# Band and tail loads of a bias table moved from GpSimd's queue to SyncE's, with memsets that release them, and a re-ordered opening

## The chip, the cores, the metric

The kernel runs on one core of one Trainium2 chip. The metric is device time in microseconds (us), the median of several executions. Ratios are the mean time of one kernel's fast runs over the mean of the other kernel's fast runs of the same rounds, with a 95% interval, so they are not quite the ratio of the medians. A run over 1.5% above the fastest of its kernel would count as slow and be left out.

## The reference

Attention with a relative-position bias over 8 batches, 8 heads, 576 positions and head size 64, then a bilinear feed-forward of 4608 tokens.

```python
scores = scale * q @ k.T                        # (8, 8, 576, 576)
bias = bias_table[bucket(abs(i - j))]           # 32 buckets x 8 heads
attn = softmax(scores + bias)
x = (attn @ v) reordered to (4608, 512)
out = ((x @ w_a) * (x @ w_b)) @ w_out           # 512 -> 1536 -> 512
```

## The kernel before

The bias enters as a factor: `exp(scores) * exp(bias)`. VectorE multiplies each block of exponentials by a slice of a band `W`, read backwards. The bands are built once: a small table is made on the chip, written to HBM by SyncE, and read back as overlapping rows, 128 partitions wide. For each head pair `hp` there is an upper part (`W0` to `W3`, 130 KB each) and a lower part (`R0` to `R3`, 160 KB each); `Wta` and `Wtb` (96 KB each) serve the tail, the last 64 positions.

```python
nc.sync.dma_start(out=tab.ap(), in_=tab_sb[0:H, :])          # the table to HBM

def load_w(hp, y0, y1):
    nc.gpsimd.dma_start(out=W_sb[hp][:, :, y0:y1],
                        in_=bass.AP(tensor=tab, offset=2 * hp * TB + y0,
                                    ap=[[NM, 128], [TB, 2], [1, y1 - y0]]))
def load_wt(hh):
    nc.gpsimd.dma_start(out=Wt_sb[64 * hh:64 * hh + 64, :, 64:256], in_=...)
```

The first two batches, the loads, and the first feed-forward units are placed by hand in one list, the opening. Each engine gets its instructions in the order of that list. `<x` is a load, `TK`/`TQ`/`TZ` are transpositions of keys, queries and tails, `S` scores, `E` exponentials (ScalarE), `M` products with `W` (VectorE), `AV`/`N`/`X` attention times values, its normalisation and transposition, `C..:D` or `:A` copies on VectorE or ScalarE, `KS`/`EK` the tail keys, `w` fills with zeros, `FA`/`FB` products with `w_a` and `w_b`.

```
<k0 <q0 <k1 <q123h0 <k23 <tk <W0 <v0 <W1 <vtb <vta <tq <W2 <R0 <v1 <Wta <q123h1 <W3 <Wtb <R1
<wa0 <k4 <wb0 <R2 <R3 <q4 ...
TK0 PC0:A TQ0 ... S001 PX0:D CQ01:A S000 E001 E000 ... S301 M001 TQ20 ... FA0a N01 HA0a ... FB0a
```

After the opening (about 70 us) a loop handles the other batches.

The softmax here doesn't subtract the row's maximum and nothing guards it: scores larger than these inputs give would overflow.

## Time and profile before

| | before |
|---|---|
| median of the first 3 runs | 414.07 us (412.92 to 414.61) |
| span of the profiled run | 412.2 us |
| first product with `wa` (`FA0a`) | 26.55 us |
| first product with `wb` (`FB0a`) | 29.44 us |
| first product with `w_out` | 70.65 us |

The lines of the profile, and how they were read, are in the prediction below.

### The profile page before, as it was taken

The page shows a single profiled execution, that of the slowest core. Times are in us where ns is not written, and L with a number is a line of the kernel's source. Part 1 is how long each engine was busy: PE and PEld are TensorE (multiplying, and loading weights), DVE is VectorE, ACT ScalarE, POOL GpSimd, SP SyncE. Part 2 cuts the span into 40 slices and gives each one's busy share as a digit, 9 for nine tenths or more (in the row PEclk, how much of TensorE's full clock was granted, in tenths as well). Part 3 has the DMA queues.
Part 4 walks back from the last instruction along what each step waited for, and adds up shares of the span by engine and source line. Part 5 has one row for each costly group of instructions (what it writes and reads, how often), then busy time and mean ns, then how long its engine had stood idle before and what let it go on. Part 6 is the DMA issues. An engine that isn't in the chain of part 4 may idle for free.

```text
span 412.2 us, 8768 instructions
## 1 busy us (share of the span) xinstructions
PE 404.5 (98%) x3473; PEld 210.0 (51%) x3473; DVE 240.8 (58%) x568; ACT 251.3 (61%) x384; POOL 133.6 (32%) x191
## 2 busy tenths in 40 slices
PE   8999999999999999999999999999999999999996
PEld 3576656455555455455444555555545554444443
DVE  3898997366745665476656764667547652421320
ACT  4998992676748665677556765767486642322321
POOL 6967547788029300960079004300000000000000
PEclk9999999999999999999999999999999999999999
DMA  8999999999979914995299709960520012002004
GB/s 104 179 202 189 206 166 144 160 193 142 87 133 159 139 34 91 155 129 90 41 161 143 116 16 126 127 92 17 117 67 16 17 40 78 0 9 95 2 2 102
DMA packets 135786, 42.05 MB, mean 102 GB/s; under 512 B 113688, under 2 KB 130968, under 8 KB 135744
## 3 DMA queue, kind: packets, MB, share of 16 engines
q0 software_dynamic: 81712, 20.27, 56.3%
q1 hardware_dynamic: 48592, 11.87, 18.6%
q10 hardware_dynamic: 5440, 9.34, 7.2%
q8 instruction: 27, 0.44, 0.5%
q14 instruction: 15, 0.12, 0.1%
HBM read 39.18 MB, written 9.45 MB: 118 GB/s over the span
## 4 chain that ended last, share of the span: by engine, by line
PE 94%; DVE 2%; ACT 2%; DMA 1%; issue 1%; ACTq 0%; POOL 0%; POOLq 0%
PE pb L633 23%; PE pa L633 23%; PE po L670 22%; PE av L569 8%; PE qk L406 7%; PE av L559 2%; PE av L563 2%; PE qkh L446 1%; PE qkt L479 1%; DMA qn<-in_q_dram 1%; PE trb L321 1%; ACT ath L452 1%; PE trb L415 1%; PE trb L609 0%; DVE ath L461 0%
## 5 line engine op out<-in xcount | busy, mean ns | idle before, releaser
L430 ACT ACTIVATE at<-qk 128x1024 bf16<-128x1024 f32 x112 | 113.3, 1028 | 27.5 <-DMA out_dram<-ob 10.3
L643 DVE TENSOR_TENSOR g<-pb,ha 128x512 bf16<-128x512 f32 (+1 forms) x114 | 75.6, 664 | 75.0 <-PE pb L633 58.9
L633 PE MATMUL pb<-xn,wb 128*128 128x512 bf16 (+1 forms) x456 | 112.1, 368 | 0.2 <-DVE g L643 0.2
L633 PE MATMUL pa<-xn,wa 128*128 128x512 bf16 (+1 forms) x456 | 112.1, 368 | 0.0
L640 ACT ACTIVATE ha<-pa 128x512 f32<-128x512 f32 (+1 forms) x114 | 66.2, 581 | 67.7 <-PE pa L633 66.2
L670 PE MATMUL po<-wo,g 128*128 128x512 bf16 x420 | 98.2, 379 | 0.0
L435 DVE TENSOR_TENSOR at<-at,W 128x1024 bf16<-128x1024 bf16 x112 | 75.1, 686 | 22.2 <-ACT at L430 22.1
L633 PEld LDWEIGHTS <-wa 128*128 128x128 bf16 x456 | 41.2, 98 | 46.3 <-issue 6.6
L633 PEld LDWEIGHTS <-wb 128*128 128x128 bf16 x456 | 40.6, 97 | 43.6 <-issue 5.2
L670 PEld LDWEIGHTS <-g 128*128 128x128 bf16 x420 | 38.9, 98 | 44.9 <-issue 2.5
L675 ACT ACTIVATE ob<-po 128x512 f32<-128x512 f32 x34 | 20.4, 600 | 39.9 <-PE po L670 33.6
L569 PE MATMUL av<-vm,at 128*128 128x65 bf16 x896 | 41.2, 193 | 0.0
L569 PEld LDWEIGHTS <-at 128*128 128x128 bf16 x896 | 37.4, 97 | 6.3
L132 POOL DMA_DIRECT2D qn<-in_q_dram x48 | 36.4, 807 | 12.0 <-PE qk L406 6.9
L170 POOL DMA_DIRECT2D vt<-in_v_dram x12 | 7.4, 620 | 98.9 <-PE av L563 98.1
L580 DVE RECIPROCAL rc<-av 128x6 f32<-128x6 f32 (+1 forms) x64 | 11.9, 186 | 45.2 <-PE av L569 40.8
L141 POOL DMA_DIRECT2D kn<-in_k_dram x48 | 36.2, 794 | 1.4 <-issue 0.7
L559 PE MATMUL av<-vt,att 128*128 128x130 bf16 x152 | 33.6, 221 | 0.0
L406 PE MATMUL qk<-QB,KB 64*128 64x512 bf16 x192 | 29.1, 381 | 0.0
L582 DVE TENSOR_TENSOR XG<-av,rc 128x384 bf16<-128x384 f32 (+2 forms) x64 | 27.2, 425 | 2.2
L506 ACT ACTIVATE att<-qkt 128x640 bf16<-128x640 f32 x24 | 16.8, 701 | 13.0 <-PE qkt L480 13.0
L559 PEld LDWEIGHTS <-att 128*128 128x128 bf16 x152 | 15.0, 98 | 6.5
(104 smaller groups left out, 327.0 us busy)
## 6 DMA issues: line engine op xcount, KB each, us to landing
out_dram<-ob ACTq DMA_DIRECT2D x31, 256.0 KB, 3.1
vn<-in_v_dram POOLq DMA_DIRECT2D x16, 256.0 KB, 5.8
kn<-in_k_dram POOLq DMA_DIRECT2D x48, 64.0 KB, 5.0
qn<-in_q_dram POOLq DMA_DIRECT2D x48, 64.0 KB, 4.4
wa<-in_moe_w_a_dram POOLq DMA_DIRECT2D x3, 512.0 KB, 7.4
wb<-in_moe_w_b_dram POOLq DMA_DIRECT2D x3, 512.0 KB, 9.2
wo<-in_moe_w_out_dram POOLq DMA_DIRECT2D x1, 1536.0 KB, 15.6
xn<-XG SPq DMA_TRANSPOSE x52, 3.0
```

Source lines behind the costliest of these rows:

```text
L132: nc.gpsimd.dma_start(out=by_tile(qn[b % 2])[:, h0 // 4, t, :, :], in_=q[b, h0:h1, 128 * t:128 * t + 128, :].transpose([1, 0, 2]))
L141: nc.gpsimd.dma_start(out=by_tile(kn[b % 2])[:, h0 // 4, t, :, :], in_=k[b, h0:h1, t:SM:NM, :].transpose([1, 0, 2]))
L406: nc.tensor.matmul(out=ps[:, hh, :], lhsT=kT[r, t, :], rhs=qT[r, :, :], start=True, stop=True)
L430: nc.scalar.activation(out=at[:, :, :], in_=ps[:, :, :], func=ACTF.Exp, scale=scale)
L435: nc.vector.tensor_tensor(out=at[:, :, :], in0=at[:, :, :], in1=w[:, :, S - 1 + t:S - 1 + t - SM:-1], op=MULT)
L559: nc.tensor.matmul(out=pav[:, slot, :, :], lhsT=weights_tail(p, jq), rhs=vt[i][:, :, hp, :], start=True, stop=True)
L569: nc.tensor.matmul(out=pav[:, slot, hh, :], lhsT=weights(p, t, hh, jq), rhs=vm[i][:, 2 * hp + hh, t, :], start=False, stop=True, skip_grou ...
L582: nc.vector.tensor_tensor(out=xg[:, jqs[0]:jqs[0] + m, :, :], in0=pav[:, 0:m, :, 0:Dh], in1=rc[:, 0:m, :].unsqueeze(3).to_broadcast([128, ...
L633: nc.tensor.matmul(out=ps[:, 0:n], lhsT=w[df // 4][:, mc, 128 * (df % 4):128 * (df % 4) + 128], rhs=xn_sb[mc][:, 512 * c + lo:512 * c + lo ...
L640: nc.scalar.activation(out=ha[:, 0:n], in_=ff["pa", df, lo][:, 0:n], func=ACTF.Copy)
L643: nc.vector.tensor_tensor(out=g_sb[df][:, lo:lo + n], in0=ff["pb", df, lo][:, 0:n], in1=ff["ha", df, lo][:, 0:n], op=MULT)
L670: nc.tensor.matmul(out=po[:, :], lhsT=g_sb[df][:, 128 * tt:128 * tt + 128], rhs=wo_sb[:, df, :], start=(df == 0), stop=(df == NDF - 1))
```

## The change

The intent: GpSimd should no longer stand for the table with other loads behind it. Six loads go to SyncE's queue. `W0` is issued as soon as the table has landed. The other five are released one by one: `>x` in the list writes one element of the load's destination on VectorE, and the load, which overwrites that element, must wait for the write. The place of `>x` in VectorE's order is thus the moment of release. The order of the other loads and of the opening changes too.

```diff
-    def load_w(hp, y0, y1):
-        nc.gpsimd.dma_start(out=W_sb[hp][:, :, y0:y1], ...)
+    def load_w(hp, y0, y1, eng):
+        eng.dma_start(out=W_sb[hp][:, :, y0:y1], ...)
     # the same for load_wt; W0 to W3, Wta, Wtb get nc.sync, R0 to R3 stay on nc.gpsimd
+        if token[0] == ">":
+            hp = "0123ab".index(token[-1])
+            x = Wt_sb[...1 element...] if hp > 3 else W_sb[hp][0:1, 0, 320:321]
+            nc.vector.memset(x, 1.0)
+            load(token[1:])
+            return
-        <k0 <q0 <k1 <q123h0 <k23 <tk <W0 <v0 <W1 <vtb <vta <tq <W2 <R0 <v1 <Wta <q123h1 <W3 <Wtb <R1
-        <wa0 <k4 <wb0 ...
+        <q0 <k0 <q123h0 <tk <k1 <k23 <v0 <W0 <tq <vtb <vta <R0 <v1 <q123h1 <R1 <wa0 <k4 <wb0 ...
+        TQ0 CQ00:A CQ01:A PC0:D TK0 CK0:D w1 S001 E001 S000 E000
+        TQ10 TZ1 TK1 PU0:D >W1 CQ10:D S011 CK1:D S101 E011 CZ1:D TQ20 TQ30 S100 E101 >W2 CQ20:D TK3
+        CQ30:D CK3:D TK2 CK2:D V0:D M001 E100 M100 KS EK >W3 M101 S201 E201 >Wtb M000 w2 S301 E301 w2
+        S200 >Wta M011 TZ0 S300 V1:D M201 CZ0:A AV10 ... FA0a HA0a FB0a ...
     # the rest of the list is re-ordered likewise (cut)
```

More of the change, by code (lines that the diff above doesn't have):

```diff
@@ L249 @@
     nc.vector.tensor_copy(out=tab_sb[0:H, c0:c0 + NR], in_=tps[0:H, 0:NR])
-    def load_w(hp, y0, y1):
-        nc.gpsimd.dma_start(out=W_sb[hp][:, :, y0:y1],
+    def load_w(hp, y0, y1, eng):
+        eng.dma_start(out=W_sb[hp][:, :, y0:y1],
                           in_=bass.AP(tensor=tab, offset=2 * hp * TB + y0,
@@ L257, with load_wt @@
     nc.sync.dma_start(out=tab.ap(), in_=tab_sb[0:H, :])
-    def load_wt(hh):
-        nc.gpsimd.dma_start(out=Wt_sb[64 * hh:64 * hh + 64, :, 64:256],
+    def load_wt(hh, eng):
+        eng.dma_start(out=Wt_sb[64 * hh:64 * hh + 64, :, 64:256],
                             in_=bass.AP(tensor=tab, offset=hh * TB + 512,
@@ L293, in load @@
         elif name[:2] == "Wt":
-            load_wt("ab".index(name[2]))
+            load_wt("ab".index(name[2]), nc.sync)
         elif name[0] in "WR":
-            load_w(int(name[1]), *((320, NY) if name[0] == "W" else (0, 320)))
+            load_w(int(name[1]), *((320, NY) if name[0] == "W" else (0, 320)), nc.sync if name in ('W0', 'W1', 'W2', 'W3', 'Wta', 'Wtb') else nc.gpsimd)
         else:
@@ L728 @@
     opening = """
-        <k0 <q0 <k1 <q123h0 <k23 <tk <W0 <v0 <W1 <vtb <vta <tq <W2 <R0 <v1 <Wta <q123h1 <W3 <Wtb <R1
-        <wa0 <k4 <wb0 <R2 <R3 <q4 <k5 <uq <q7 <q5 <wa1 <wb1 <k6 <uk <vt1b <k7 <vb1a <vb1b <vt1a <wa2 <q6
-        <wb2 <wo TK0 PC0:A TQ0 PF1:D PX1:D PV1:A PU0:D CK0:A CQ00:D w1 S001 PX0:D CQ01:A S000 E001 E000
-        w1 TQ30 PC1:D TK1 CK1:D TQ10 CQ10:D S011 E011 CQ30:D TK3 S100 E100 TZ1 CK3:D S301 M001 TQ20
-        PV0:D TK2 E301 S101 E101 CQ20:D CK2:D w1 S200 E200 CZ1:D M000 w1 KS w1 S201 EK w2 S010 E201 V0:D
@@ L734 @@
-        M101 TZ0 M100 M200 M201 AV00 N00 CZ0:A AV10 E010 X00 CX00:A S300 E300 N10 T0 V1:D X10 CX10:A
-        M010 ET0 AV20 TQ11 TQ21 M011 N20 CQ11:A S110 S111 CQ21:A E110 X20 M301 TQ31 M300 AV30 T1 PW:D
-        MT0 AV01 CX20:D M110 E111 N30 ET1 X30 M111 CQ31:A T2 ET2 S210 CX30:D E210 PF0:A LH FA0a N01 HA0a
-        MT1 TK4 X01 T3 AV11 ET3 CX01:D S211 PU1:D FB0a FA1a E211 CK4:D HA1a N11 X11 G0a M210 S310 MT2
-        CX11:A E310 FB1a G1a S311 FA2a HA2a TQ4 M211 CQ4:A FB2a AV21 E311 FA3a HA3a TQ5 MT3 M310 S43 S42
@@ L739 @@
-        CQ5:A G2a FB3a N21 M311 TK5 E43 E42 TZ0x G3a CZ0x:D AV31 LV CK5:D N31 FA4a HA4a X21 TQ7 CQ7:A
-        S41 E41 S52 E52 CX21:D FB4a FA5a HA5a X31 G4a TK6 M43 FB5a CX31:D S40 E40 S53 G5a FA0b FB0b
-        CK6:D M41 TZ1x HA0b G0b CZ1x:D S51 FA1b FB1b E53 M53 HA1b G1b E51 TK7 CK7:D M40 FA2b HA2b S50
-        E50 FB2b FA3b G2b HA3b V2:D T4 FB3b FA4b V3:D ET4 G3b S70 E70 M42 MT4 M52 HA4b FB4b G4b TQ6 T5
-        ET5 M50 CQ6:A AV40 N40 MT5 M51 FA5b S71 E71 HA5b S73 FB5b AV41 G5b M70 N41 S72 E73 FA6f E72 T6
@@ L744 @@
-        M73 M71 HA6f FB6f G6f AV50 N50 S62 ET6 MT6 E62 S61 FA7f HA7f M62 AV51 N51 TH S60 E61 M61 FB7f
-        G7f E60 M60 S63 E63 M63 FA8f HA8f M72 T7 FB8f G8f AV60 N60 ET7 MT7 FA9f HA9f FB9f G9f AV70 FA10f
-        FB10f N70 HA10f G10f AV71 FA11f N71 FB11f X71 HA11f G11f AV61 N61 X70 FO00 FO01 FO02 HO0 CX70:D
-        CX71:D
+        <q0 <k0 <q123h0 <tk <k1 <k23 <v0 <W0 <tq <vtb <vta <R0 <v1 <q123h1 <R1 <wa0 <k4 <wb0 <R2 <R3 <q4
+        <uq <k5 <q5 <wa1 <q7 <wb1 <k7 <uk <q6 <vb1a <k6 <vt1b <vb1b <vt1a <wa2 <wb2 <wo PC1:D PF0:A
@@ new lines @@
+        PX1:D PF1:D PX0:A PV0:D PV1:A PU1:A TQ0 CQ00:A CQ01:A PC0:D TK0 CK0:D w1 S001 E001 S000 E000
+        TQ10 TZ1 TK1 PU0:D >W1 CQ10:D S011 CK1:D S101 E011 CZ1:D TQ20 TQ30 S100 E101 >W2 CQ20:D TK3
+        CQ30:D CK3:D TK2 CK2:D V0:D M001 E100 M100 KS EK >W3 M101 S201 E201 >Wtb M000 w2 S301 E301 w2
+        S200 >Wta M011 TZ0 S300 V1:D M201 CZ0:A AV10 E200 N10 E300 AV00 N00 M200 TQ31 CQ31:A M301 S010
+        E010 M300 TQ11 TQ21 LH CQ21:A T0 CQ11:A M010 AV20 ET0 X00 N20 CX00:A S110 S111 AV30 PW:D X10 MT0
@@ new lines @@
+        E110 N30 X20 CX10:D E111 M111 T1 CX20:A AV01 N01 X30 ET1 TK4 CX30:A T2 ET2 S210 FA0a HA0a FB0a
+        M110 MT1 X01 CX01:D T3 E210 CK4:A FA1a G0a HA1a AV11 MT2 ET3 N11 S211 E211 M210 FB1a G1a FA2a
+        HA2a TQ4 X11 CQ4:A S311 E311 S310 M211 FB2a FA3a MT3 HA3a CX11:D M311 AV21 TQ5 E310 G2a TK5 N21
+        CK5:D CQ5:A S42 E42 S43 E43 M310 FB3a FA4a HA4a G3a TQ7 TZ0x CZ0x:D AV31 LV N31 S41 S52 FB4a
+        CQ7:A E41 X21 X31 FA5a G4a E52 CX21:D HA5a CX31:D FB5a S40 E40 S53 G5a FA0b HA0b FB0b M43 M52
@@ new lines @@
+        E53 TK6 TK7 G0b FA1b CK6:D M53 S51 FB1b HA1b G1b E51 FA2b HA2b TZ1x CK7:A S50 M42 E50 FB2b FA3b
+        HA3b CZ1x:D T4 G2b TQ6 M41 M40 FB3b FA4b S70 G3b ET4 V2:D HA4b MT4 FB4b T5 E70 ET5 M51 AV40 S71
+        E71 FA5b V3:D G4b N40 FB5b MT5 M50 AV41 N41 HA5b G5b S72 S73 CQ6:A FA6f AV50 E72 M71 M72 N50 T6
+        M70 E73 FB6f HA6f G6f ET6 S62 MT6 FA7f E62 M62 AV51 HA7f S61 E61 S60 N51 TH E60 M61 FB7f G7f M60
+        S63 E63 FA8f M63 T7 HA8f FB8f ET7 M73 AV60 G8f FA9f HA9f FB9f MT7 N60 AV70 FA10f G9f FB10f N70
@@ L748 @@
+        HA10f AV71 FA11f G10f FB11f N71 X71 HA11f G11f AV61 X70 N61 CX70:D FO00 FO01 FO02 CX71:D HO0
     """
@@ L757, in step @@
                     if token[1] == "a" else None)
+            return
+        if token[0] == ">":
+            hp = "0123ab".index(token[-1])
+            x = Wt_sb[64 * (hp - 4):64 * (hp - 4) + 1, 0, 64:65] if hp > 3 else W_sb[hp][0:1, 0, 320:321]
+            nc.vector.memset(x, 1.0)
+            load(token[1:])
             return
```

## The prediction

> **What bounds the kernel now.** I read the page from the whole to the part: busy times and the chain that ended last, then busy time in stretches of ten microseconds, then the waits of GpSimd, then the order of time on ScalarE, GpSimd and TensorE in the opening (the hand-written list that the change replaces; it ends near 73 us). First the whole page:
>
> ```profile
> span 412.2 us, 8768 instructions
> PE 404.5 (98%) x3473; PEld 210.0 (51%) x3473; DVE 240.8 (58%) x568; ACT 251.3 (61%) x384; POOL 133.6 (32%) x191
> PE 94%; DVE 2%; ACT 2%; DMA 1%; issue 1%; ACTq 0%; POOL 0%; POOLq 0%
> ```
>
> 94% of the chain of 412.2 us is TensorE itself. What is not TensorE is some 25 us at most, so the question is where those lie. Busy time by stretch (columns: length, PE, weight loads, DVE, ACT, POOL, granted clock, DMA share, GB/s):
>
> ```profile
> 0.00:10.00 10.00, 7.95 (x58) 3.23 (x58) 3.74 (x19) 5.14 (x8) 6.29 (x13) 1.00 0.84 103
> 10.00:20.00 10.00, 9.29 (x123) 5.27 (x120) 8.74 (x21) 8.84 (x12) 10.00 (x15) 1.00 1.17 183
> 20.00:30.00 10.00, 9.27 (x172) 7.22 (x170) 9.48 (x29) 9.03 (x14) 6.27 (x10) 1.00 1.25 196
> 30.00:40.00 10.00, 10.00 (x142) 6.97 (x140) 8.90 (x29) 8.87 (x16) 7.45 (x11) 1.00 1.38 189
> 40.00:50.00 10.00, 10.00 (x118) 6.65 (x116) 9.37 (x24) 9.48 (x17) 6.34 (x9) 1.00 1.31 204
> ```
>
> From 30 us on TensorE has no idle time at all, and the chain lies on TensorE without a break from 22.3 us. Before that it is not the bound, though its busy share looks high (matmuls overlap, and seven of them are fills with zeros). Between 10 and 26 us ScalarE and VectorE are the busy ones (88 to 95%), GpSimd issues loads without a pause from 10 to 20 us, and the DMA engines move nearly what they move later. So the opening has three near-limits: exponentials, vector work, and arrival of loads. Two waits and the issue times of GpSimd show what the change aims at (waits: total, times, longest; then its order of time: start, duration):
>
> ```profile
> POOL W L252 <- DMA bias_tab<-wo: 2.7, 1, 2.7
> POOL qn L123 <- DMA wa<-in_moe_w_a_dram: 1.8, 1, 1.8
> ...
> 8.31 0.72 POOL L252 DMA_DIRECT2D W<-bias_tab  x1 [2.66 <-DMA bias_tab<-wo]
> 9.02 0.78 POOL L123 DMA_DIRECT2D vn<-in_v_dram  x1
> 17.92 0.88 POOL L270 DMA_DIRECT2D wa<-in_moe_w_a_dram  x1
> 19.39 0.89 POOL L270 DMA_DIRECT2D wb<-in_moe_w_b_dram  x1
> ```
>
> The first load of band rows needs the bias table in HBM, which lands at 8.3 us; everything behind it on GpSimd, the v load first, stands until then. Last, ScalarE's exponentials, and TensorE where the feed-forward products begin:
>
> ```profile
> 8.01 1.94 ACT L452 ACTIVATE ath<-qkh 128x1024 bf16<-128x1024 f32 x2 [0.28 <-PE qkh L446]
> 10.79 3.05 ACT L452 ACTIVATE ath<-qkh 128x1024 bf16<-128x1024 f32 x3 [0.84 <-PE qkh L446]
> 13.99 1.94 ACT L452 ACTIVATE ath<-qkh 128x1024 bf16<-128x1024 f32 x2 [0.16 <-PE qkh L446]
> ...
> 26.55 0.61 PE L633 MATMUL pa<-xn,wa 128*128 128x256 bf16 x4
> ...
> 29.44 0.61 PE L633 MATMUL pb<-xn,wb 128*128 128x256 bf16 x4
> ```
>
> The first product needs the normalised, transposed outputs of all four head pairs for the first 256 rows. From there TensorE always has something to do. **The change can therefore gain only what it takes off the time before the first products**; the work after them is the same.
>
> **What the Trainium skill says.** "DMA: Bandwidth & Descriptors", section "Issuing engines are not separate DMA queues": loads issued from different engines share the same 16 DMA engines, and a second issuer saves only the issue time of the sequencer. The trace agrees on what an issue costs: 0.72 to 0.89 us each on GpSimd, and fifteen of them fill 10 to 20 us. The same page, "Two DMAs through the same engine are not ordered": a load that reads what another wrote must be held by the issuing engine until the first one's semaphore is full. That is the 2.7 us wait; on SyncE the wait stays but holds only SyncE. The same page, "Latency and other measured facts": the first byte comes sooner on the hardware path (about 0.6 us) than on GpSimd's (about 1 us). This trace has 1.7 us from issue to landing for small loads on SyncE against 3.1 us at best on GpSimd, but for other sizes, so it does not settle what a 130 KB band row will take.
>
> **The change part by part.**
>
> 1. *Six issues leave GpSimd* (four W, two Wt): 6 x 0.73 = 4.4 us of issue, plus the 2.7 us wait = 7.1 us. With v issued at about 5.6 instead of 9.02 us, wa0 could be issued at 17.9 - 7.1 = 10.8 us. But at most eight GpSimd loads are in flight (each waits for the one eight places before, in the built program; the 1.8 us wait on wa above is that), so wa0 (the fifteenth) waits for v, the seventh: about 13 us. Issue thus stops being the limit and arrival takes over.
>
> 2. *What arrival gains.* All the same bytes go before wa0: adding the sizes of section 6, 3272 KB up to wa0 and 3912 KB up to wb0 (k4's 128 KB and wb0's 512 KB). Before, wb0 is issued at 19.39 and lands 9.3 us later, at 28.7 us; wa0 lands at 25.3. The engines ran at 110 GB/s from 9 to 11 us, 161 from 14 to 16, and 122 from 20 to 22, against some 185 about them: (75 + 24 + 63) x 2 us = 324 KB, at 190 KB a microsecond 1.7 us, if every hole is filled. Estimate: wa0 at 23.7, wb0 at 27.0 to 27.3 us. The v load gains less: W0 and W1 now share the engines with it from 8.4 us, so I expect it at about 13 instead of 13.5 us.
>
> 3. *The order of exponentials.* The third exponential now takes the second half of pair 0, whose queries are already there, instead of waiting for pair 1; this is where the 0.84 us idle before 10.79 us goes. Adding ScalarE's work in the new order from 8.0 us to the copy that releases the first product: 12 exponentials x 0.93, tail keys 0.95, two tail exponentials x 0.9, about nine copies x 0.34 (ten at most) = 11.2 + 1.0 + 1.8 + 3.1 = 17.1 us, so 25.0 us without idle time. VectorE comes out the same: v copied by 13.8, then twelve products with the bias x 0.62, v's second half 0.7, four normalisations x 0.55, and 1.5 us of tail and copies give 24 to 25 us. First product at about 25.0 instead of 26.55: 1.5 us sooner.
>
> 4. *What the new order gives back.* In the old list some 2 us of other TensorE work (a tail product 0.4, one attention-value group 0.95, three transposes 0.3, one score group 0.3) lie between the first product with wa and the first with wb. The new list puts the wb product directly behind it. At 25.5 us wb0 has not landed by point 2, so TensorE stands until about 27.1. The product ends at 27.6, and the 1.95 us of skipped work still has to be done: 29.6 us for the state that the old kernel reaches at 29.98. Net 0.4 us if wb0 lands at 27.1; 2.0 us if it lands by 25.5.
>
> 5. *What it adds.* Five one-element memsets on VectorE, 0.06 us each by the small memsets at 1.7 us: 0.3 us of a busy engine, contained in point 3 within its error. Two fewer zero fills on TensorE, which filled waits. Both off the path.
>
> Sum: between -0.4 and -2.0 us, middle -1.2 us, a bit more for the skew towards filled holes: **412.7 us** against 414.07.
>
> **The rivals.** (a) *The loads on SyncE overtake.* Each queue gets its turn at the engines, so band rows may push back v and wa rather than fill holes. For it: DMA share over 1.1 from 11 us on. Against it: the later rows are held back by memsets behind vector work at 11 to 16 us, which is what these are for. Then the first product stays at 26.5 us or later and the time at 414 to 415. (b) *Issue was the whole limit.* If 200 GB/s are reached from 5 us on, wb0 lands by 25.5 us and ScalarE's 1.5 us and part of the fills come through: 411.5 to 412. (c) *VectorE becomes the bound.* A late W2, W3 or Wt (each gated) would stop its queue; each such stop moves the first product by its full length: up to 2 us lost, 414 to 416. (d) *Nothing moves*, because TensorE after 30 us is full anyway: it speaks only about work after 30 us; a shift of the start of the full stretch goes through to the end, so I give it little.
>
> **Range and chances.** 2% is 8.3 us. For that the full stretch would have to start at 18 us, yet ScalarE alone has 17 us of work from 8 us on; so faster by over 2% is nearly excluded. Slower by 2% needs 8 us of new waits early on, more than any load is late. The before runs spread over 1.7 us, which widens the range: 411.0 to 414.4 us. Faster 0.02, within 0.97, slower 0.01.
>
> **What would show each step right or wrong.** Point 1: GpSimd's wait on the bias table is gone ahead of v, and wa is issued at 12.5 to 14 us. Point 2: issue plus time to landing gives 23.7 for wa0 and 27 for wb0. Point 3: no idle over 0.3 us on ScalarE from 8 to 18 us, first product at 25.0. Point 4: idle time of 1 to 2 us on TensorE ahead of the first wb product, released by that load. Stretches after 40 us must look the same but for a shift. The prediction is wrong if the band rows land so late that VectorE waits for them, or if a changed stretch after 50 us (loads of batch 2, their transposes on SyncE) loses or gains time on its own.

## The result, and the profile after

The changed kernel took 415.81 us (median of 6, 414.18 to 416.17) against 413.92 us for before (6 runs): a ratio of 1.0039, interval 1.0017 to 1.0061. It is slower by 1.9 us in the medians (1.6 us by the ratio), outside the predicted range. The loss is small, but clear of the noise of these runs.

The page of after: span, busy times, and the shares of the chain that ended last.

```profile
span 414.0 us, 8724 instructions
PE 400.5 (97%) x3420; PEld 210.1 (51%) x3471; DVE 239.0 (58%) x571; ACT 251.2 (61%) x386; POOL 129.6 (31%) x185
PE 88%; DMA 4%; ACT 2%; POOL 2%; issue 2%; DVE 1%; ACTq 0%; DVEq 0%; POOLq 0%
```

TensorE's share of the chain fell from 94 to 88%, and DMA and GpSimd took some of it. The loads that this chain names are of queries and keys (2% each); the releasers in it are inferred, and the argument below rests on the waits instead. (TensorE's instruction count differs mostly because records of matmuls are missing; the weight loads, 3471 against 3473, show the two fewer fills.) By stretch (columns as in the prediction):

```profile
10.00:20.00 10.00, 8.67 (x133) 5.19 (x132) 7.64 (x23) 8.92 (x12) 6.90 (x10) 1.00 1.37 214
20.00:30.00 10.00, 6.80 (x120) 5.10 (x112) 7.13 (x20) 6.33 (x11) 4.73 (x8) 1.00 1.31 219
```

More bytes move than before (214 and 219 GB/s against 183 and 196), GpSimd is no longer full from 10 to 20 us, and yet from 20 to 30 us every compute engine does less: VectorE 7.1 us instead of 9.5, ScalarE 6.3 instead of 9.0, TensorE 6.8 instead of 9.3. What VectorE waits for from 8 to 30 us (total, times, longest):

```profile
DVE ath L461 <- DMA W<-bias_tab: 2.5, 3, 1.4
...
DVE Wt L313 <- DMA Wt<-bias_tab: 1.2, 1, 1.2
```

Before, VectorE never waited for a band row. Here are its products with the bands and the memsets that release them, in order of time:

```profile
13.99 0.69 DVE L461 TENSOR_TENSOR ath<-ath,W 128x1024 bf16<-128x1024 bf16 x1 [0.29 <-DMA W<-bias_tab]
15.51 1.31 DVE L461 TENSOR_TENSOR ath<-ath,W 128x1024 bf16<-128x1024 bf16 x2 [0.82 <-DMA W<-bias_tab]
16.15 0.06 DVE L761 MEMSET W<- 1x1 bf16 x1
16.88 0.06 DVE L761 MEMSET Wt<- 1x1 bf16 x1
...
17.60 0.06 DVE L761 MEMSET Wt<- 1x1 bf16 x1
...
22.29 1.90 DVE L461 TENSOR_TENSOR ath<-ath,W 128x1024 bf16<-128x1024 bf16 x3 [1.38 <-DMA W<-bias_tab]
...
26.02 0.23 DVE L313 COPY Wt<-Wt 128x256 bf16<-128x256 bf16 x1 [1.21 <-DMA Wt<-bias_tab]
```

`W0` costs 0.29 us, `W1` 0.82, `W3` 1.38, the tail band 1.21: together 3.70 us. The memset for `W3` stands in VectorE's order behind a product that itself waits for `W1`. It is executed at 16.15 us, and the row it releases is needed at 20.9. On TensorE the first products come to lie here:

```profile
29.44 0.61 PE L633 MATMUL pa<-xn,wa 128*128 128x256 bf16 x4
29.89 0.60 PE L633 MATMUL pb<-xn,wb 128*128 128x256 bf16 x4
```

So `FA0a` is 2.89 us later (29.44 against 26.55). From `FA0a` to the end the new list needs 384.6 us (414.03 - 29.44) against 385.6 (412.16 - 26.55): 1.0 us less. A key transposition of 0.3 us that now stands ahead of `FA0a` is a part of that; the rest was not looked into. Together they make 1.9 us of span, which is the loss. Two questions follow: why were the rows late, and is the list to blame as well?

### The profile page after: what moved, and what is told of

Read it like the earlier page. It is cut to its first block, busy times and chain, and to the rows that moved or that the text cites. A ratio compares the mean times of both kernels' runs of the same rounds, so it can differ in the third digit from the quotient of the medians.

```text
span 414.0 us, 8724 instructions
## 1 busy us (share of the span) xinstructions
PE 400.5 (97%) x3420; PEld 210.1 (51%) x3471; DVE 239.0 (58%) x571; ACT 251.2 (61%) x386; POOL 129.6 (31%) x185
## 4 chain that ended last, share of the span: by engine, by line
PE 88%; DMA 4%; ACT 2%; POOL 2%; issue 2%; DVE 1%; ACTq 0%; DVEq 0%; POOLq 0%
PE pa L633 22%; PE pb L633 22%; PE po L670 22%; PE av L569 7%; PE qk L406 7%; PE av L559 2%; DMA qn<-in_q_dram 2%; DMA kn<-in_k_dram 2%; PE av L563 2%; PE qkt L479 1%; ACT at L430 1%; PE trb L415 1%; POOL tlc L158 1%; DVE ath L461 0%; POOL kn L123 0%
## 5 line engine op out<-in xcount | busy, mean ns | idle before, releaser
L633 PE MATMUL pa<-xn,wa 128*128 128x512 bf16 (+1 forms) x440 | 110.8, 368 | 0.7
L670 PE MATMUL po<-wo,g 128*128 128x512 bf16 x403 | 95.5, 379 | 0.8
```

The costliest lines, as they stand in the source:

```text
L633: nc.tensor.matmul(out=ps[:, 0:n], lhsT=w[df // 4][:, mc, 128 * (df % 4):128 * (df % 4) + 128], rhs=xn_sb[mc][:, 512 * c + lo:512 * c + lo ...
L670: nc.tensor.matmul(out=po[:, :], lhsT=g_sb[df][:, 128 * tt:128 * tt + 128], rhs=wo_sb[:, df, :], start=(df == 0), stop=(df == NDF - 1))
```

## The experiments

Four theories. **Backlog:** the rows are late because GpSimd, freed from its wait, keeps the engines filled with up to eight loads issued earlier. **Path:** issuing such rows from SyncE is slow in itself. **Gates:** the memsets release the rows too late. **Order:** the new list is slower whatever the loads do. All experiments gave correct results. The runs of before were shared within each set (the experiments are four sets, each on another chip).

| run | median, us | before, us | ratio (95%) | `FA0a`, us |
|---|---|---|---|---|
| after | 415.81 | 413.92 | 1.0039 (1.0017 to 1.0061) | 29.4 |
| queue alone | 415.85 | 413.82 | 1.0049 (1.0030 to 1.0069) | 29.4 |
| order alone | 415.10 | 413.82 | 1.0031 (1.0013 to 1.0049) | 27.5 |
| after, no gates | 414.45 | 413.82 | 1.0016 (0.9992 to 1.0040) | 27.8 |
| after, GpSimd held | 416.26 | 413.82 | 1.0063 (1.0037 to 1.0090) | 30.7 |
| queue alone, GpSimd held | 413.68 | 414.43 | 0.9992 (0.9968 to 1.0016) | 27.1 |
| after, gates early | 413.11 | 414.43 | 0.9975 (0.9959 to 0.9992) | 26.8 |
| after, rows split | 413.95 | 414.43 | 0.9997 (0.9980 to 1.0014) | 26.8 |
| after again | 414.53 | 413.93 | 1.0031 (1.0005 to 1.0058) | 28.3 |
| order alone, loads fitted | 414.80 | 413.93 | 1.0013 (0.9999 to 1.0027) | 28.4 |
| gates early, work moved | 416.15 | 413.93 | 1.0050 (1.0036 to 1.0064) | 29.0 |
| the same, rows first | 416.46 | 413.93 | 1.0052 (1.0032 to 1.0073) | 30.0 |
| gates early again | 413.33 | 413.78 | 0.9988 (0.9968 to 1.0008) | 26.6 |

`FA0a` is from one profiled run each; the two runs of after differ by 1.1 us, so a difference of under 1 us in that column proves nothing.

### Queue alone

```diff
 # before, with:
-        nc.gpsimd.dma_start(out=W_sb[hp]...)      # W0 to W3, Wta, Wtb
+        nc.sync.dma_start(out=W_sb[hp]...)        # no memsets, list of before
```

> The list of before, word for word, with the six band and tail loads issued on SyncE and no memsets to release them. Four theories. Backlog: SyncE's rows are late because GpSimd, no longer held by the table, keeps eight loads ahead of them in the engines; then W0 takes 5 to 6 us from issue to landing here too, the first product with the bias (11.7 us in before) stands until about 13.5 to 14, and the time is 414.8 to 416. Path: SyncE's way of issuing such rows is slow in itself; same numbers here. Gates: rows are late because the memsets release them late; there are none here, so 413 to 414. Order: the new list of computations costs the time; here 413 to 414.5, like before.

`W0`, issued at 8.08 us, landed at 14.28. VectorE waited for it in one piece:

```profile
DVE ath L461 <- DMA W<-bias_tab: 3.4, 1, 3.4
```

That wait also held the key copies behind it in VectorE's order, and TensorE stood 2.8 us for one of them. The time rose by 2.0 us. So the queue alone does harm, without gates and without a new order. Backlog and path are both still possible.

### Order alone

```diff
 # after, with every row on GpSimd, no memsets:
-<k23 <v0 <W0 <tq <vtb <vta <R0 <v1 <q123h1 <R1 <wa0
+<k23 <W0 <v0 <W1 <tq <vtb <vta <W2 <R0 <v1 <Wta <q123h1 <W3 <Wtb <R1 <wa0
```

> The list of after without the memsets, all band and tail loads on GpSimd again at the relative places that they had in before (W0 ahead of the first v half, W1 behind it, and so on). Backlog, path and gates: rows land 3.1 to 4.7 us after their issue as in before, no wait of VectorE on W or Wt over 0.3 us, first product with wa at 25 to 26.5 us, time 412.3 to 414. Order: 415 to 416, as after.

A miss for the first three theories: VectorE waited for no row, but it stood 2.2 us for the second half of v and TensorE 1.9 us for queries, which the new list uses earlier than the old places deliver them. 415.10 us is what the order theory gave. (TensorE also stood 0.5 us for `wb0` here, the wait that point 4 of the prediction expected.) The new list is no gain when its loads come at the old places. It needs earlier loads, so list and load order can't be judged apart.

### After without gates

```diff
-<v0 <W0 <tq         ... >W1 ... >W2 ... >W3 ... >Wtb ... >Wta
+<v0 <W0 <W1 <W2 <W3 <Wtb <Wta <tq
```

> After, with W0, W1, W2, W3, Wtb and Wta issued on SyncE one behind the other as soon as the table has landed, no memsets. Gates: W3 and Wt have landed long before their use, the waits of 1.4 us (W3) and 1.2 us (Wt) go, and with them most of the loss: 413 to 414.3. Backlog or path: W0 and W1 come no sooner than in after (13.9 and 15.4 us), v's second half and the queries come later because more bytes go ahead of them, so half of the gain is given back: 414.5 to 415.8.

`W0` landed at 13.77 us (13.90 in after), `W3` at 17.89, the last tail row at 19.77, and no wait on a row over 0.3 us remained. In their place VectorE waited 1.2 us for v (18.47 us instead of 17.10) and TensorE 1.6 us for the queries (19.83 instead of 18.46). `FA0a` came 1.6 us sooner than in after; the median of 414.45 lies between the two forecasts, and the interval includes 1. Rows released all at once push back other loads, so gates have a use. Whether it is their place that is wrong, a later run tests.

### After with GpSimd held

```diff
+        if name == "hold":     # 16 dead bytes that need the table
+            nc.gpsimd.dma_start(out=hold_sb[:, :], in_=bass.AP(tensor=tab, offset=0, ap=[[8, 1], [1, 8]]))
     # hold_sb's own line and a return are cut here
-<k23 <v0 <W0 <tq
+<k23 <hold <v0 <W0 <tq
```

> After, with one dead load of 16 bytes of the table put on GpSimd ahead of the first v half, so that GpSimd stands until the table has landed, as it did in before; band rows stay on SyncE with their memsets. Backlog: W0 now meets nearly empty engines and lands 3 to 4 us after its issue (by 11 to 11.8 us instead of 13.9), W1 by 12.7; VectorE's waits on W0 and W1 go, v comes at about 13.5; time 414.3 to 415.3. Path: W0 still takes 6 us, and v is late on top: 416 or more.

This tells backlog from path. `W0` was issued at 8.20 and landed at 11.12 us (2.9 us), `W1` at 11.53. The packets that started, by queue (q0 is GpSimd's, q1 SyncE's; the share adds up the times of packets that overlap, so it can pass 100%), first for after from 8.0 to 10.8 us, where two rows had been issued at 7.83 and 8.28 (and a third at 10.76):

```profile
## 3 DMA queue, kind: packets, MB, share of 16 engines
q0 software_dynamic: 871, 0.42, 125.8%
```

then for after with GpSimd held, from 8.2 to 11.1 us:

```profile
## 3 DMA queue, kind: packets, MB, share of 16 engines
q0 software_dynamic: 411, 0.19, 54.6%
q1 hardware_dynamic: 539, 0.26, 37.5%
...
W<-bias_tab SPq DMA_DIRECT2D x3, 130.0 KB, 2.9
```

In after not one packet of SyncE's rows started in 2.8 us, while 871 of GpSimd's did; the first started at 11.13 us, 3.3 us after the issue. With GpSimd held the first started at 9.24 us, 1.0 us after the issue. The path theory falls, the backlog stands.

The time, though, was 416.26 us, which is what the path theory had forecast (416 or more); only the landings tell the two apart. GpSimd's loads all came later: the first v half was issued at 8.99 us instead of 5.58. `W3`, issued at 16.09 us just behind `wa0`, `k4` and `wb0`, took 7.8 us.

```profile
DVE ath L466 <- DMA W<-bias_tab: 2.9, 1, 2.9
...
DVE Wt L318 <- DMA Wt<-bias_tab: 0.9, 1, 0.9
```

The waits on `W0` and `W1` were gone, and the kernel was still slow. In this kernel, then, the costly rows are `W3` and the tail.

### Queue alone, with GpSimd held

```diff
 # queue alone, with the same dead load:
-<tk <W0 <v0 <W1
+<tk <hold <W0 <v0 <W1
```

> The queue alone (the list of before, six rows on SyncE, no memsets) with the dead load of the table on GpSimd ahead of the first v half, so that GpSimd stands until the table has landed, as in before. If the wait that the change removed was what gave the first row empty engines: W0 lands about 3 us after its issue (11 to 11.5 us, against 14.3 without the hold), VectorE's 3.4 us wait on W0 goes, the first product with wa comes at 26 to 27 us (29.4 without), and the time is 413 to 414.2, 1.7 to 2.8 us under the queue alone. If rows on SyncE are slow for another reason in the old list, the time stays at 415 to 416.

`W0` landed at 10.80 us, 3.1 us after its issue. VectorE waited for no row; its list of waits begins:

```profile
DVE KT L318 <- PE trk L326: 2.6, 1, 2.6
DVE vm L318 <- DMA vn<-in_v_dram: 1.4, 1, 1.4
```

413.68 us, ratio 0.9992 against 1.0049 (another set of rounds; the intervals do not meet). One added load that nobody reads, put there to make GpSimd stand for the table again, brings back what the queue move lost. The wait that the change removed had kept the engines nearly free for the first row.

### After with the gates early

```diff
-CQ30:D CK3:D TK2 CK2:D V0:D M001 E100 M100 KS EK >W3 M101 S201 E201 >Wtb M000 w2 S301 E301 w2
-S200 >Wta M011
+CQ30:D CK3:D TK2 CK2:D >W3 >Wtb >Wta V0:D M001 E100 M100 KS EK M101 S201 E201 M000 w2 S301 E301 w2
+S200 M011
```

> After, with the three last memsets (W3, Wtb, Wta) ahead of the first v copy and the first product with the bias, so that none stands behind an instruction that itself waits for a row. Cascade of gates: the three are issued at 12.5 to 14 us instead of 16.3 to 17.8 and land by 19 to 21 us instead of 22.3 to 25.9; VectorE's waits of 1.4 us on W3 and 1.2 us on Wt go; v and the queries keep their times within 0.5 us; first product with wa at 26 to 27 us instead of 29.4; wb0 lands near 27; time 412.3 to 413.8, below after by 2 us or more. If the issue time of the gates does not matter: W3 lands past 21.5 us and the time stays above 415.

Three memsets moved, nothing else. VectorE in order of time:

```profile
12.82 0.06 DVE L761 MEMSET W<- 1x1 bf16 x1
12.96 0.06 DVE L761 MEMSET Wt<- 1x1 bf16 x1
13.06 0.42 DVE L313 COPY vm<-vn 128x1024 bf16<-128x1024 bf16 x1
13.07 0.06 DVE L761 MEMSET Wt<- 1x1 bf16 x1
14.00 0.69 DVE L461 TENSOR_TENSOR ath<-ath,W 128x1024 bf16<-128x1024 bf16 x1 [0.52 <-DMA W<-bias_tab]
15.31 2.50 DVE L461 TENSOR_TENSOR ath<-ath,W 128x1024 bf16<-128x1024 bf16 x4 [0.62 <-DMA W<-bias_tab]
...
20.00 2.50 DVE L461 TENSOR_TENSOR ath<-ath,W 128x1024 bf16<-128x1024 bf16 x4
...
23.03 0.22 DVE L313 COPY Wt<-Wt 128x256 bf16<-128x256 bf16 x1
```

`W3` landed at 19.29 us (22.27 in after), the tail rows at 21.11 and 22.56 (24.52 and 25.93). The transfer of `W3` is no faster (6.4 us against 6.0); it is issued 3.3 us sooner (12.93 against 16.26). The waits on these rows are gone, those on `W0` and `W1` remain (1.1 us together, as in after). Not all was as expected: v's second half and the queries came 0.8 and 1.2 us later than in after, where 0.5 was allowed, and TensorE stood 1.5 us for the queries. `FA0a` at 26.76 us, 413.11 us, ratio 0.9975. This is the main cause of the loss in after: the place of three memsets is worth 0.64% here, if the ratios to before are set side by side (1.0039 and 0.9975, from different sets of rounds).

### After with the rows split

```diff
-<v1 <q123h1 <R1 <wa0          # W3, Wtb, Wta on SyncE, released by memsets
+<v1 <q123h1 <W3 <Wtb <Wta <R1 <wa0      # on GpSimd; W0, W1, W2 stay on SyncE
```

> After, with W0, W1, W2 on SyncE as in after and W3, Wtb, Wta back on GpSimd ahead of R1 and wa0, so that they go ahead of the first feed-forward weights in GpSimd's own row of loads. If what made W3 and Wt late is the megabyte of wa0, k4 and wb0 that is issued before them: W3 lands at 18.5 to 20.5, Wt by 21.5, wa0 at about 23 (21.5 in after), wb0 near 27 (25.9 in after), first product with wa at 26 to 27 us, time 412.5 to 414. If it is their late issue alone, the same; if neither, above 415.

`W3` landed at 19.31 us, the tail rows at 20.00 and 20.31, `wa0` at 23.01; `FA0a` 26.77. These three rows can go by either queue, if they are issued in time. Whether they must go ahead of `wa0`, `k4` and `wb0` the run does not tell: both explanations forecast the same, and with the early gates the tail rows were issued behind `wa0` (13.39 and 14.18 against 12.97 us) and still came in time. The time of 413.95 us is in the expected range; it equals before within its interval.

### After again, and three tries

> After once more, unchanged, on the chip of the next three runs. If the loss is real and not of one chip: 415 to 416.3, ratio to before 1.003 to 1.006, VectorE's waits on W1, W3 and Wt again 0.6 to 1.5 us each, first product with wa at 28.8 to 30 us.

The loss is real (interval 1.0005 to 1.0058), but of the six runs four were at 414.1 to 414.7 us and two at 417.1 and 417.4, so its size varies from run to run. It is also smaller than expected: 414.53 us and `FA0a` at 28.34 us lie below the forecast ranges. In the profiled run VectorE waited 1.5 us on `W3` and 0.7 on the tail, and 1.0 us on `W0` but only 0.3 on `W1`, which is not as expected.

```diff
 # order alone, with v1 and the queries ahead of the later rows:
-<W1 <tq <vtb <vta <W2 <R0 <v1 <Wta <q123h1 <W3 <Wtb <R1
+<W1 <tq <vtb <vta <R0 <v1 <q123h1 <W2 <W3 <Wtb <Wta <R1
```

> The new list with all rows on GpSimd, as in the order alone, but v's second half and the queries ahead of W2, W3, Wtb and Wta, as the new list uses them. In the order alone VectorE stood 2.2 us for v and TensorE 1.9 us for the queries. If it was the misfit of load places and list that cost the order alone its time: v lands by 17 us, the queries by 18.5, both waits fall under 0.7 us, first product with wa at 25.5 to 26.8 us (27.5), time 412.5 to 413.8. If the new list is slower in itself: 415 as the order alone.

A miss: v landed at 17.38 us and the queries at 18.38, near the expected 17 and 18.5, yet waits of VectorE on v (1.8 us in two) and on rows (1.2 us in two), and of TensorE on the queries (1.6) and on the tail load `tq` (1.0) remained, and 414.80 us lies between the two forecasts. Whether the new list can gain with all rows on GpSimd stays open.

```diff
 # gates early, with:
-S100 E101 >W2 CQ20:D TK3 CQ30:D CK3:D ... M100 KS EK M101
+S100 E101 >W2 CQ20:D CQ30:D KS EK TK3 CK3:D ... M100 M101
-M200 TQ31 CQ31:A M301 S010 E010 M300 ... T0 ... ET0
+M200 S010 E010 T0 ET0 TQ31 CQ31:A M301 M300 ...
-PW:D  CX10:D
+PW:A  CX10:A
```

> The early gates, and work moved where it waited: the tail keys ahead of the third key transposition; one score group, the first tail product and their exponentials ahead of the query transposition that stood 1.5 us for its load; two small copies from VectorE to ScalarE. If VectorE, busy without a stop from 15.3 us on, bounds the first product: 26.0 to 26.5 us (26.8 with the early gates), 412.3 to 413.2. If ScalarE is the bound after all: up to 1 us sooner, 411.8 to 412.6. If the copies only load ScalarE: as the early gates, 413 to 413.8.

A clear miss, 416.15 us. With the tail keys ahead of the third key transposition, VectorE stood 1.7 us for that transposition, and the v copy and all products with the bands stood behind it (the first at 15.0 us instead of 14.0). Later TensorE waited 1.2 us for a query copy on ScalarE. Several edits at once, so only the first effect is assigned.

```diff
-<v0 <W0 <tq <vtb <vta <R0 <v1
+<v0 <W0 <R0 <tq <vtb <vta <v1      # on top of the kernel above
```

> The kernel of the run before with W0's other half ahead of the tail loads on GpSimd, so that GpSimd stands for the table from 6.3 to 7.7 us and W0 and W1 meet a shorter backlog. By the backlog: W0 and W1 land 0.7 to 1.3 us sooner (12.6 to 13.2 and 13.9 to 14.5 us), tail loads 1 us later; VectorE starts its products 0.5 to 1 us sooner and the first product with wa comes 0.3 to 1 us sooner: 411.8 to 413. If the backlog in front is only k and v: no change over 0.3 us.

`W0` came at 12.77 and `W1` at 14.34 us, 1.4 and 0.6 us sooner than in the run before it: the backlog again. But the first product came no sooner (29.99 us against 29.02), and the time was 416.46 us, a miss: the loss made by the kernel beneath hides any use.

### Gates early again

> The early gates once more, unchanged, in a new set of rounds. If the gain over both kernels is real: ratio to before 0.996 to 0.999, 412.4 to 413.6 us, no wait of VectorE on W3 or Wt, first product with wa at 26.3 to 27.3 us. If the first set was luck: ratio 0.9995 to 1.002.

413.33 us, ratio 0.9988; no wait on `W3` or the tail, `FA0a` at 26.64 us. Against after, which was never in the same rounds, its ratio is lower in both sets (0.9975 and 0.9988, against 1.0039 and 1.0031), by 0.64 and 0.43%; the intervals of the second pair overlap slightly. Against before it was lower both times, but this interval (0.9968 to 1.0008) includes 1, so a gain over before of 0.5 to 1 us is likely rather than shown. It is the best kernel found.

## Why the prediction was wrong

- **What bounds the kernel** was right for one list: a shift of the first product goes through to the end. From `FA0a` to the end it is 384.6 to 384.8 us in every run of the new list with rows on SyncE (385.0 and 385.6 with all rows on GpSimd), and 385.3 to 385.6 in the old list. It was wrong in that the change "can therefore gain only what it takes off the time before the first products": the early gates have `FA0a` no sooner than before (26.76 and 26.64 against 26.55 us), and what they gain lies behind it. Nor is TensorE always busy there: in after it is idle for 0.75 us from 30 to 70 us, in before never.
- **Point 1** (issues leave GpSimd) was right: the v load is issued at 5.58 us, and `wa0` at 12.46, just ahead of the forecast 12.5 to 14.
- **Point 2** (arrival) failed in the sentence "All the same bytes go before wa0". `W3` and the two tail rows, 322 KB, landed behind `wa0` in after (22.27 to 25.93 against 21.46 us). At the prediction's 190 KB a microsecond these are 1.7 us, most of the 2.2 us by which `wa0` came sooner than forecast (21.5 instead of 23.7; `wb0` 25.9 instead of 27.0). The forecast treated SyncE's rows as loads that take a share at once, and worked out arrival for v and the weights, but for none of the rows. The v load, which the rows were to slow down, came at 12.2 us instead of 13.
- **Point 3** (VectorE's sum of 24 to 25 us) is the step that made the time wrong. It added up work and left out 3.70 us of waits for rows, the sign that the prediction itself had named for being wrong. Without them `FA0a` would be at about 29.44 - 3.70 = 25.7 us (an estimate), near the forecast 25.0. That closeness is in part luck: the terms as written add up to 25.6 us, not 24 to 25; the trace has ten products ahead of the fourth normalisation, not twelve; and from the end of that (27.40 us) to `FA0a` another 2.0 us pass, which the sum lacks. ScalarE had 0.8 us gaps at 10 and 13 us too, which point 3 excluded, but it started 0.5 us sooner (7.46 instead of 8.01) and in the end waited 3.5 us for VectorE.
- **Point 4** (the `wb` product stands for its load) was wrong in this kernel: `wb0` lay ready 4 us ahead. With all rows on GpSimd (order alone) the wait did show, 0.5 us.
- **The rivals.** (c), "VectorE becomes the bound", is what happened, with its 414 to 416 us; it named W3 and Wt, though not W0 and W1, and was given too little weight. What it did not see is the cascade: the gate of `W3` stands behind a product that waits for `W1`. (a) had the mechanism the wrong way round: it feared that SyncE's rows overtake GpSimd's loads, and it took the memsets for a safeguard. (b) nearly had the arrival (`wb0` at 25.9 us, 214 GB/s), but not the time.

The shared cause, shown by the two runs with GpSimd held and by the early gates: when a row lands is set by when it is issued and by what the engines still have to move then. `W0` took 2.9 and 3.1 us from issue to landing with GpSimd held, 6.1 and 6.2 us without. It is not strictly first come, first served: in after `W3`, issued at 16.26 us, landed at 22.27, ahead of `wb0`, issued at 13.92 and landed at 25.88. The 2.7 us in which GpSimd stood for the table looked like a loss; in the old list it left the engines to the row that VectorE needed first.

What the Trainium skill says in "DMA: Bandwidth & Descriptors", "Issuing engines are not separate DMA queues", that all issuers share the same 16 DMA engines and a second one saves only issue time, agrees with these runs: issued from SyncE behind GpSimd's loads, the six rows took 6.0 to 8.2 us to land in after, against 3.1 to 4.7 us from GpSimd in before.

## What to carry to other kernels

Before you remove a wait on a queue of loads, ask what the engines serve in that time: a stalled issuer can be what lets the urgent transfer go through. A load that must be released in time needs its gate ahead of any instruction that itself waits for such a load, early by the time to landing under load (6 to 8 us here, not the 3 us seen with little queued). And work out the arrival of every load that the busiest engine reads, not only of those that the change seems to favour.

## What the Trainium skill lacked or had wrong

- "DMA: Bandwidth & Descriptors", section "Queues, rings and completion order", says that each DMA engine takes turns between the queues it has work for, packet by packet. By that one would expect SyncE's row to start soon beside GpSimd's loads. The runs show a start 3.3 us after the issue (11.13 against 7.83 us) and no packet of it between 8.0 and 10.8 us, with 871 packets of GpSimd's loads started; with GpSimd held, 1.0 us. This does not show the page wrong, since the two do not count the same: the trace's packets are single transfers (two rows of 130 KB are 512 of 520 bytes and 32 of 4 bytes), while a packet of the page is 9 to 17 of them as a rule and 64 at most. 871 are 54 for each engine, some turns at the usual size and less than one at the largest. Where the row waits in that time the trace does not tell. Once under way, both queues do interleave (1288 and 494 packets from 11 to 14 us).
- The same page, section "Latency and other measured facts", gives a sooner first byte for the hardware path. For a 130 KB row on engines with little queued, SyncE's path took 2.9 to 3.1 us from issue to landing (not to the first byte), GpSimd's 3.1 us in two runs and 3.6 in one: little to plan with. The section has HBM's own latency at high load, but no figure for a load behind a backlog of others, where SyncE's six loads took 6.0 to 8.2 us in after.
- No page that was read warns that a load released by an instruction of a compute engine inherits that engine's waits; here it moved the release of `W3` and the tail rows by 3.3 to 4.5 us (memsets at 16.15 to 17.60 us against 12.82 to 13.07) and cost 0.4 to 0.6%.
